# Source order for all engines and row pairs (gate, gate, value, value) from batch 2 on, in a fused attention, GLU and soft mixture-of-experts kernel

## The chip, the cores and the metric

The kernel runs on one core of a Trainium2 chip. The metric is the device time of one execution in microseconds (us). One execution was taken with the hardware profiler; all trace rows in this document are from that execution.

## What is computed

The reference has three parts, one behind the other. `B, H, S, Ns, D = 8, 8, 512, 32, 64`, all float32.

```python
# 1: cross reads between tokens x (B,H,S,D) and states (B,H,Ns,D)
a     = softmax(x @ state.T / sqrt(D), over states);  xread = a @ state
a2    = softmax(state @ x.T / sqrt(D), over tokens);  sread = a2 @ x
x     = concat([xread, sread], rows) as (4352 tokens, 512)
# 2: gated linear unit behind an RMS norm, d_ff = 1536
xn    = x / rms(x) * rms_g
h     = silu(xn @ w_gate) * (xn @ w_val);             x = h @ w_out
# 3: soft mixture of experts, 8 experts with 4 slots each
logits   = x @ phi
d        = softmax(logits, over tokens);  slot_in = d.T @ x
slot_out = relu(slot_in @ w1[e]) @ w2[e]   per expert
out      = softmax(logits, over slots) @ slot_out
```

## The kernel before

**Tiles and stages.** The 512 tokens of one batch element ("batch" below, 0 to 7) make one group `g` of four row tiles of 128. The kernel never forms `xread`: since `xread @ w = a @ (state @ w)`, it first multiplies the 32 states by a 512-column block of the gate or value weights (the state product, `sw`, line 531; its result is the tile `wp`, in a high and a low part), and then multiplies the attention weights `A` with it (`main_mm`, line 557). d_ff is cut into three blocks `c` of 512 columns. So a batch has 12 units `(g, c, t)`. A unit has a gate row and a value row of six matmuls each. ScalarE turns the gate row into `sg` (SiLU, `main_silu`, line 572), VectorE makes `h = value * rinv * sg` (`main_h`, line 577).

Stage 0 holds units of batches 0 and 1 and most of the weight preparation, stage 1 the rest of batch 1, stages 2 to 7 one batch each. Then come six halves for the 256 rows of `sread` (`w_split` at line 784 cuts weights for them into two parts on ScalarE and VectorE), the experts and the output. From stage 8 on the expert weights are streamed in.

**Small work between main rows.** In stages 2 to 7 the main rows stand in blocks of 24 matmuls (two units), and behind each block stands a burst of small work, written out by hand in `steady(g)`, bursts 0 to 5. It holds:

- `turn(c, t)` = `h_T` (line 586): four 128x128 transposes of `h` on TensorE into a `misc` bank, then a copy to `hT` on ScalarE, or on VectorE when the third argument is true. `lg_mm` (line 598) multiplies four turned tiles with `w_out @ phi` for the logits;
- `post1`, `post2`, `post_exp`, `post3`, `slot_h` (lines 622 to 705): the running softmax over tokens of the batch before. `post_exp` makes `E`, `post3` transposes `E` and `L`, `slot_h` adds to `acc`; `sacc` is the running sum (line 664). `c_exp`, `c_norm` (lines 707, 712) do the softmax over slots;
- `sw(g, c, gv)` for the blocks of columns that come next. Its two PSUM banks are emptied by a cast on ScalarE (line 545) and a subtraction on VectorE (line 546) each;
- the attention of the next batch `nb` and the one after it `nn`: `att_a3` (scores `sT`), `att_a4` (transposed scores `a`, maxima `rm`, `cm`, `ncm`), `att_exp`, `att_norm`, `att_b1` to `att_b4`, `att_z`, `att_gram`, `att_q`, `att_v`, `att_ss`, `rinv_from` (lines 225 to 526). `att_q`, `att_v`, `att_ss` and `rinv` give the RMS factor from the Gram matrix of the states;
- one piece of weight conversion (`wload`, `wconv`, lines 161 and 195): two ScalarE passes, three VectorE operations and one GpSimd addition per half, and a store.

Work for the other engines alone is put on units by `at(u, slot, f)`: slot 1 of unit `u` is run between its gate and value row, slot 2 behind its value row.

**Buffers.** PSUM has three banks `mm` for main rows, four banks `misc` for all small work and one bank `lg`. SBUF tiles of 8 KB a partition come from one pool `k8` with 19 buffers; attention tiles from `k4` with 5.

**What sets the order.** The framework takes instructions per engine from a heap by priority, so an engine's order can differ from the source. In stages 2 to 7 the order of TensorE alone is given by the source:

```python
pe_order.enter_context(tc.manual_schedule(engines={mybir.EngineType.PE}))
```

On the other engines only instructions marked with `tc.keep_in_program_order` keep their place (some ScalarE exponentials, `att_z`, `att_g`). All VectorE work and nearly all of ScalarE's, GpSimd's and the DMA queue's (SyncE) is placed by the heap. SyncE issues every load and store of these stages in one queue.

Of the kernel before, what the change touches and what calls it, by code (L numbers as in the profile page):

```python
# [20 lines left out]
def kernel(  # L21
# [87 lines left out]

    def transpose(o, i):  # L110
        nc.tensor.transpose(o, i, ident)  # L111
# [64 lines left out]
    def wconv_begin():  # L176
# [12 lines left out]
        if pinned:  # L189
            tc.keep_in_program_order(ins)  # L190
        ins = nc.scalar.activation(out=rnd, in_=lo.bitcast(U32), func=AF.Copy, scale=2.0 ** -29)  # L191
        if pinned:
            tc.keep_in_program_order(ins)
        begun.append((gv, c, j, d2, dst, hi, rnd))

    def wconv(n):
        for _ in range(n):
            if not begun:
                wconv_begin()
            gv, c, j, d2, dst, hi, rnd = begun.pop(0)  # L200
            a = dst.bitcast(I32)
            hs = [slice(0, 512), slice(512, 1024)]
            for h in hs:
                nc.vector.tensor_scalar(  # L204
                    out=dst[:, h], in0=dst[:, h], scalar1=EXP_LO, scalar2=EXP_HI,
                    op0=ALU.max, op1=ALU.min,
                )
                nc.vector.tensor_scalar(  # L208
                    out=a[:, h], in0=a[:, h], scalar1=3, scalar2=0x3FFFFFF8,
                    op0=ALU.logical_shift_left, op1=ALU.bitwise_and,  # L210
                )
                nc.vector.scalar_tensor_tensor(  # L212
                    out=a[:, h], in0=hi[:, h], scalar=-0x40000000, in1=a[:, h],
                    op0=ALU.bitwise_and, op1=ALU.bitwise_or,
                )
                nc.gpsimd.tensor_tensor(  # L216
                    out=a[:, h], in0=a[:, h], in1=rnd[:, h], op=ALU.add
                )
            if gv == 2:
                WOT[c, j] = d2  # L220
            if gv == 3:
                r0 = c * 512 + 2 * j * P
                nc.sync.dma_start(
                    out=w_out32[r0 : r0 + 2 * P, :].rearrange("(k p) d -> p k d", p=P), in_=d2
                )

    def att_g(b):
# [7 lines left out]
        if b > 0:  # L237
            tc.keep_in_program_order(ins)
# [26 lines left out]
    def att_a4(b):  # L265
        sT = T[b, "sT"]
        if b > 0:
# [11 lines left out]
            if b > 3:  # L279
                cm = T[b, "cm"]  # L280
                nc.vector.reduce_max(cm, sT, axis=AX.X)
                nc.vector.tensor_scalar(
                    out=T[b, "ncm"], in0=cm, scalar1=-scale, scalar2=None, op0=ALU.mult
# [333 lines left out]
    Q = {}  # L617
# [881 lines left out]
```

## Time and profile before

| | us |
|---|---|
| median of 3 runs | 665.63 |
| lowest and highest | 663.20, 666.14 |
| the profiled execution | 666.31 |
| its span, first to last instruction | 664.5 |
| TensorE busy | 615.8 (93%) |
| VectorE, ScalarE, GpSimd busy | 438.9 (66%), 346.5 (52%), 157.3 (24%) |
| mean granted TensorE clock | 0.961 |

The span is one execution on the chip; the profiled time has 1.8 us around it. Busy time of TensorE (PE) is a modelled number: matmuls overlap, so the distance from the start of one group of matmuls to the start of the next tells more than its busy share. The page's line of the granted clock shows full speed in nearly all slices between the start and the end of the kernel.

### The profile page before, as it was taken

Reading aid. Unit: us, or ns where it says so; the run is one execution under the profiler, and the core shown is the slowest. Engines: PE = TensorE matmul, PEld = TensorE weight load, DVE = VectorE, ACT = ScalarE, POOL = GpSimd, SP = SyncE. Lnnn points to the kernel's source line nnn. Section 1 sums busy time; section 2 is a strip of 40 time slices with the busy share of each in tenths; the row PEclk is TensorE's granted clock in tenths of the full one; section 3 lists DMA queues with packets and bytes.
Section 4 is the critical chain, followed back from the end, with each engine's and each line's share of the span. In section 5 each row is a group of like instructions: output and inputs, shape, how many; then the busy total and the mean of one; then the engine's idle time right before and its main releaser. Section 6 shows DMA issues by size and latency. Waiting matters only on the chain.

```text
span 664.5 us, 11190 instructions
## 1 busy us (share of the span) xinstructions
PE 615.8 (93%) x4432; PEld 387.5 (58%) x4432; DVE 438.9 (66%) x876; ACT 346.5 (52%) x552; POOL 157.3 (24%) x178
## 2 busy tenths in 40 slices
PE   6787989899998999999999999999999999999990
PEld 4435655356565566566656666666666777653350
DVE  6969899676578676856867685786765365252160
ACT  5457784475268447544844763484346476311170
POOL 2635464442031411401141041113000000003420
PEclk9588998899999999999999999999999999999996
DMA  9950064231020410041040104300270327999857
GB/s 354 417 206 1 1 241 190 77 127 51 18 62 35 163 33 33 1 163 64 1 154 14 60 1 159 128 1 34 92 288 3 126 86 269 312 337 396 311 205 332
DMA packets 32715, 92.14 MB, mean 139 GB/s; under 512 B 1816, under 2 KB 3224, under 8 KB 29848
## 3 DMA queue, kind: packets, MB, share of 16 engines
q1 hardware_dynamic: 32376, 91.36, 37.3%
q8 instruction: 35, 0.57, 0.3%
q14 instruction: 16, 0.13, 0.1%
q10 hardware_dynamic: 288, 0.07, 0.0%
HBM read 79.37 MB, written 12.06 MB: 138 GB/s over the span
## 4 chain that ended last, share of the span: by engine, by line
PE 75%; DVE 15%; ACT 5%; issue 2%; DMA 1%; POOL 0%; DVEq 0%; ACTq 0%
PE mm L85 43%; PE misc L85 18%; PE misc L111 9%; PE lg L85 3%; DVE w L204 2%; PE so L85 2%; DVE wp L546 2%; DVE w L212 2%; DVE h L582 1%; DVE w L208 1%; DVE wo L204 1%; DVE wo L212 1%; DMA raw_t<-in_w_gate_dram 1%; ACT hT L593 1%; ACT wp L545 1%
## 5 line engine op out<-in xcount | busy, mean ns | idle before, releaser
L85 PE MATMUL mm<-wp,A 128*128 128x512 f32 x1152 | 285.8, 400 | 2.9 <-DVE h L582 2.2
L85 PEld LDWEIGHTS mm<-wp,A 128*128 128x128 f32 x1152 | 213.3, 190 | 73.8 <-issue 23.8
L582 DVE SCALAR_TENSOR_TENSOR h<-mm,rinv,sg 128x512 f32<-128x512 f32 x102 | 76.0, 747 | 88.2 <-PE mm L85 82.0
L574 ACT ACTIVATE sg<-mm,rinv 128x512 f32<-128x512 f32 x102 | 70.7, 693 | 103.3 <-PE mm L85 88.9
L545 ACT CAST wp<-misc 128x512 fp32r<-128x512 f32 x96 | 51.5, 591 | 68.1 <-PE misc L85 68.1
L546 DVE TENSOR_TENSOR wp<-misc,wp 128x512 fp32r<-128x512 f32 x96 | 62.6, 684 | 23.2 <-ACT wp L545 22.8
L85 PE MATMUL misc<-w,stTg 64*32 64x512 f32 x768 | 67.7, 637 | 7.9 <-POOL w L216 5.1
L111 PEld LDWEIGHTS misc<-ident,h 128*128 128x128 f32 x408 | 44.9, 140 | 37.4 <-DVE h L582 13.9
L593 ACT COPY hT<-misc 128x512 f32<-128x512 f32 x81 | 45.3, 592 | 38.1 <-PE misc L111 32.4
L111 PE MATMUL misc<-ident,h 128*128 128x128 f32 x408 | 58.3, 279 | 5.8 <-DVE wp L546 5.1
L216 POOL TENSOR_TENSOR w<-w,raw 128x512 int32<-128x512 int32 x20 | 28.3, 1428 | 29.6 <-issue 7.3
L519 POOL TENSOR_TENSOR rinv<-ri,rs_magic 128x4 int32<-128x4 int32 (+1 forms) x9 | 1.8, 197 | 131.4 <-DVE ri L515 131.4
L85 PE MATMUL mm<-wh,xsg 128*128 128x512 f32 x96 | 31.8, 400 | 0.0
L216 POOL TENSOR_TENSOR wo<-wo,raw 128x512 int32<-128x512 int32 x18 | 24.7, 1384 | 22.6 <-DVE wo L212 7.0
L85 PEld LDWEIGHTS misc<-w,stTg 64*32 64x32 f32 x768 | 11.0, 107 | 31.4 <-issue 10.9
L476 POOL TENSOR_TENSOR A<-aT,A 128x1024 fp32r<-128x1024 f32 x7 | 16.9, 2408 | 47.5 <-ACT A L475 47.5
L85 PE MATMUL lg<-hT,wphi 128*32 128x512 f32 (+1 forms) x216 | 27.5, 579 | 0.0
L85 PE MATMUL misc<-h,ET 128*32 128x512 f32 x204 | 26.4, 596 | 0.0
L1245 POOL MEMSET sinE<- 128x512 f32 x2 | 1.0, 524 | 105.7 <-PE mm L85 95.6
L574 ACT ACT_TABLE_LOAD x18 | 23.1, 1283 | 0.8 <-PE mm L85 0.5
L191 ACT ACTIVATE raw<-raw 128x1024 int32<-128x1024 uint32 x19 | 21.9, 1155 | 0.0
L85 PEld LDWEIGHTS mm<-wh,xsg 128*128 128x128 f32 x96 | 17.9, 188 | 6.6 <-issue 3.1
(223 smaller groups left out, 852.6 us busy)
## 6 DMA issues: line engine op xcount, KB each, us to landing
ew<-in_w_dram SPq DMA_DIRECT2D x27, 1024.0 KB, 7.7
xT<-in_x_t_dram SPq DMA_DIRECT2D x8, 1024.0 KB, 7.4
xn<-in_x_n_dram SPq DMA_DIRECT2D x8, 1024.0 KB, 6.0
raw<-in_w_val_dram SPq DMA_DIRECT2D x6, 1024.0 KB, 15.8
raw<-in_w_out_dram SPq DMA_DIRECT2D x6, 1024.0 KB, 5.3
out_dram<-ob SPq DMA_DIRECT2D x6, 1024.0 KB, 10.7
ew_w<-in_w_dram SPq DMA_DIRECT2D x5, 1024.0 KB, 10.5
raw<-in_w_gate_dram SPq DMA_DIRECT2D x4, 1024.0 KB, 13.7
```

What stands on the lines that cost most here:

```text
L85: nc.tensor.matmul(out=o, lhsT=lhsT, rhs=rhs, start=start, stop=stop)
L111: nc.tensor.transpose(o, i, ident)
L191: ins = nc.scalar.activation(out=rnd, in_=lo.bitcast(U32), func=AF.Copy, scale=2.0 ** -29)
L204: nc.vector.tensor_scalar(out=dst[:, h], in0=dst[:, h], scalar1=EXP_LO, scalar2=EXP_HI, op0=ALU.max, op1=ALU.min,)
L212: nc.vector.scalar_tensor_tensor(out=a[:, h], in0=hi[:, h], scalar=-0x40000000, in1=a[:, h], op0=ALU.bitwise_and, op1=ALU.bitwise_or,)
L216: nc.gpsimd.tensor_tensor(out=a[:, h], in0=a[:, h], in1=rnd[:, h], op=ALU.add)
L476: nc.gpsimd.tensor_tensor(out=A[:, :, 1, :], in0=aT, in1=A[:, :, 0, :].bitcast(F32), op=ALU.subtract)
L545: nc.scalar.copy(t[:, r, 0, :], ps)
L546: nc.vector.tensor_tensor(out=t[:, r, 1, :], in0=ps, in1=t[:, r, 0, :].bitcast(F32), op=ALU.subtract)
L574: nc.scalar.activation(out=sg, in_=ps, func=AF.Silu, scale=RINV[g][:, t : t + 1])
L582: nc.vector.scalar_tensor_tensor(out=HH[g, c][:, t, :], in0=ps, scalar=RINV[g][:, t : t + 1], in1=sg, op0=ALU.mult, op1=ALU.mult,)
L593: (nc.vector.tensor_copy if on_dve else nc.scalar.copy)(HT[g, c][:, :, t * P : (t + 1) * P], ps.rearrange("p (q n) -> p q n", q=4))
```

## The change

From stage 2 to the end of stage 7, `manual_schedule()` without an engine list gives the order of every engine by the source; the single marks (`keep`) are off there. The two units of a block run gate, gate, value, value in place of gate, value, gate, value; slot 1 of the first unit now stands behind both gate rows and slot 1 of the second between the two value rows. In the bursts every `sw` moves to the end of its burst, each `turn` is paired, and `att_gram` goes from burst 0 to burst 1. `post_exp` and `c_exp` leave burst 0 for slot 1 of unit 2; `att_exp` goes from unit 1 to unit 0; `load_xt` from unit 8 to unit 5; `att_v` from burst 4 to unit 8; `att_z` and `att_a4` to unit 10; `c_norm` from unit 2 to unit 6; the weight conversion is cut in two halves, in burst 2 and at unit 6. Four functions are cut off others so that they can stand elsewhere: `att_cm`, `att_rs`, `post_sum`, `sread_split`; `sread_prep2` moves from the end of stage 6 to burst 0 of stage 7. No operation is added or removed.

The diff, cut to its core (the bodies of `wconv_half`, `att_cm`, `att_rs`, `post_sum` and `sread_split` are lines of the functions before):

```diff
+    by_hand = []
+    def keep(ins):
+        if not by_hand:
+            tc.keep_in_program_order(ins)
...
+    def wconv_half(i):
...
+    def att_cm(b):
+        cm = T[b, "cm"]
+        nc.vector.reduce_max(cm, T[b, "sT"], axis=AX.X)
+        nc.vector.tensor_scalar(
+            out=T[b, "ncm"], in0=cm, scalar1=-scale, scalar2=None, op0=ALU.mult
+        )
...
-            tc.keep_in_program_order(ins)
+            keep(ins)
+        if not by_hand:
+            att_rs(b)
...
         b = bursts[0]
         if g > 2:
             b += [(lg_mm, g - 1, 2, 3), (post1, g - 1)]
-        b += [turn(0, 0, True), (sw, g, 1, 0), (post2, g - 1)]
-        if not last:
-            b += [(att_gram, nb)]
-        b += [(post_exp, g - 1), (c_exp, g - 2, True)]
+        b += [turn(0, 0, True), turn(0, 1, True), (post2, g - 1), (sw, g, 1, 0)]
+        if last:
+            b += [(sread_prep2,)]
         b = bursts[1]
         if 2 < g < B - 1:
             b += [(att_b2, g)]
-        b += [(sw, g, 1, 1), turn(0, 1, True), (post3, g - 1), turn(0, 2)]
+        if not last:
+            b += [(att_gram, nb)]
+        b += [turn(0, 2, True), (post3, g - 1)]
         if not last:
             b += [(att_b1, nb)]
+        b += [turn(0, 3), (post_sum, g - 1), (sw, g, 1, 1)]
         b = bursts[2]
-        b += [turn(0, 3), turn(1, 0)] + [(slot_h, g - 1, i) for i in range(NC)]
+        b += [(slot_h, g - 1, i) for i in range(NC)]
+        if not last:
+            b += [(lg_mm, g, 0, 3)]
+        if g == B - 2:
+            b += [(att_b2, nb)]
         if 2 < g < B - 1:
             b += [(att_b3, g)]
-        if g == B - 2:
-            b += [(att_b2, nb)]
-        b += [(lg_mm, g, 0, 3), (sw, g, 2, 0)]
+        b += [turn(1, 0), turn(1, 1)]
+        if not last:
+            b += [(wconv_half, 0)]
+        b += [(sw, g, 2, 0)]
         b = bursts[3]
-        b += [(sw, g, 2, 1)]
         if not last:
             b += [(att_q, nb, 0), (att_q, nb, 1)]
-        b += [turn(1, 1), turn(1, 2)]
+        else:
+            b += [(lg_mm, g, 0, 3)]
+        b += [turn(1, 2), turn(1, 3)]
         if g == B - 2:
             b += [(att_b3, nb)]
+        b += [(sw, g, 2, 1)]
         b = bursts[4]
         if nn < B:
             b += [(att_a3, nn)]
-        b += [turn(1, 3)]
-        if not last:
-            b += [(att_v, nb), (att_ss, nb), (rinv, nb), (sw, nb, 0, 0)]
-        else:
-            b += [turn(2, 0)]
+        if last:
+            b += [(lg_mm, g, 1, 3)]
         if g == B - 2:
             b += [(sread_sum,)]
+        b += [turn(2, 0, True), turn(2, 1)]
+        if not last:
+            b += [(att_ss, nb), (rinv, nb)]
+        if not last:
+            b += [(sw, nb, 0, 0)]
         b = bursts[5]
         if not last:
-            b += [(sw, nb, 0, 1), turn(2, 0), (lg_mm, g, 1, 3), turn(2, 1), turn(2, 2), turn(2, 3, True)]
-            if g == B - 2:
-                b += [(sread_prep2,)]
+            b += [(lg_mm, g, 1, 3), turn(2, 2), turn(2, 3, True)]
+            if nn < B and nn > 3:
+                b += [(att_cm, nn)]
+            b += [(sw, nb, 0, 1)]
             ended.add(g)
         else:
-            b += [turn(2, 1), (lg_mm, g, 1, 3), turn(2, 2)]
+            b += [turn(2, 2)]
...
-        at(2, 1, c_norm, g - 2)
+        at(6, 1, c_norm, g - 2)
         if not last:
+            at(0, 1, att_exp, nb)
+            at(0, 1, wload, 1)
+            at(2, 1, att_rs, nb)
+            at(2, 1, att_norm, nb)
+        at(2, 1, post_exp, g - 1)
+        at(2, 1, c_exp, g - 2)
+        if not last:
+            at(4, 1, att_b4, nb)
+            at(4, 1, wconv_begin)
+            at(6, 1, wconv_half, 1)
+            at(6, 1, att_g, nb)
             at(1 if g == B - 2 else 7, 1, load_xn, nb)
-            at(1, 1, att_exp, nb, True)
-            at(2, 1, att_norm, nb)
-            at(4, 1, att_b4, nb)
-            at(6, 1, att_g, nb)
-            at(1, 1, wload, 1)
-            at(4, 1, wconv, 1)
+            at(8, 1, att_v, nb)
         if nn < B:
-            at(8, 1, load_xt, nn)
-            at(9, 1, att_z, nn)
-            at(11, 1, att_a4, nn)
+            at(5, 2, load_xt, nn)
+            at(10, 1, att_a4, nn)
+            at(10, 1, att_z, nn)
...
+            at(6, 1, sread_split)
             at(11, 1, w_split, 0, 0)
...
-                pe_order.enter_context(tc.manual_schedule(engines={mybir.EngineType.PE}))
+                by_hand.append(pe_order.enter_context(tc.manual_schedule()))
+                by_hand.append(1)
...
             if s > 1:
                 if u % 2:
-                    for f, *a in bursts[u // 2]:
+                    continue
+                pair = units[u : u + 2]
+                sgs = []
+                for k, (_, c, t) in enumerate(pair):
+                    ps = main_mm(g, c, t, 0)
+                    sgs.append(main_silu(g, c, t, ps))
...
+                for k, (_, c, t) in enumerate(pair):
+                    for f, a in plan.pop((base + u + k, 1), []):
                         f(*a)
+                    psv = main_mm(g, c, t, 1)
+                    main_h(g, c, t, psv, sgs[k])
...
+                    for f, a in plan.pop((base + u + k, 2), []):
+                        f(*a)
+                for f, *a in bursts[u // 2]:
+                    f(*a)
...
         if s == B - 1:
             pe_order.close()
+            by_hand.clear()
```

## Rows read from the trace of the kernel before

**Rows 1.** Stretches: start:end, length, busy PE, PEld, DVE, ACT, POOL, clock, DMA share, GB/s.
```profile
186.70:249.40 62.70, 60.53 (x433) 38.07 (x425) 48.95 (x98) 35.17 (x56) 16.52 (x14) 1.00 0.24 79
308.20:367.00 58.80, 58.11 (x461) 37.92 (x457) 42.07 (x84) 32.44 (x53) 11.87 (x11) 1.00 0.19 65
425.80:483.80 58.00, 57.23 (x510) 38.24 (x502) 40.38 (x84) 30.58 (x49) 8.80 (x8) 1.00 0.21 75
483.80:538.40 54.60, 54.00 (x353) 37.27 (x346) 29.18 (x65) 29.82 (x50) 0.20 (x1) 1.00 0.30 112
...
593.00:629.00 36.00, 35.48 (x316) 13.69 (x309) 7.96 (x32) 3.31 (x6) 11.71 (x35) 1.00 0.99 376
```

**Rows 2.** Timeline of TensorE in batch 4: start us, length us, line, tiles, count, [idle before].
```profile
327.00 0.27 PE L677 MATMUL misc<-ident,E 128*128 128x128 f32 x1
327.11 0.27 PE L678 MATMUL misc<-ident,L 128*128 128x128 f32 x1
327.99 0.66 PE L111 MATMUL misc<-ident,h 128*128 128x128 f32 x4 [0.60 <-DVE wp L546]
328.58 1.40 PE L111 MATMUL misc<-ident,sT 128*128 128x128 f32 x8
329.73 5.71 PE L85 MATMUL mm<-wp,A 128*128 128x512 f32 x24
335.28 1.03 PE L111 MATMUL misc<-ident,h 128*128 128x128 f32 x8
336.24 2.78 PE L85 MATMUL misc<-h,ET 128*32 128x512 f32 x24
...
340.21 1.09 PE L85 MATMUL misc<-w,stTg 64*32 64x512 f32 x16
341.23 5.74 PE L85 MATMUL mm<-wp,A 128*128 128x512 f32 x24
346.90 1.09 PE L85 MATMUL misc<-w,stTg 64*32 64x512 f32 x16
...
357.93 1.46 PE L85 MATMUL misc<-w,stTg 64*32 64x512 f32 x16
359.32 5.73 PE L85 MATMUL mm<-wp,A 128*128 128x512 f32 x24
```

**Rows 3.** The same view in batch 2.
```profile
200.91 5.98 PE L85 MATMUL mm<-wp,A 128*128 128x512 f32 x24
206.82 1.09 PE L85 MATMUL misc<-w,stTg 64*32 64x512 f32 x16
...
208.44 0.27 PE L678 MATMUL misc<-ident,L 128*128 128x128 f32 x1
210.80 0.65 PE L111 MATMUL misc<-ident,h 128*128 128x128 f32 x4 [2.08 <-DVE wp L546]
```

**Rows 4.** Waits of TensorE from 186.7 to 538 us: us in total, times, longest.
```profile
PE misc L111 <- DVE wp L546: 5.1, 6, 2.1
```

**Rows 5.** Timeline of ScalarE and VectorE behind the state product of 340.21.
```profile
341.34 1.08 ACT L545 CAST wp<-misc 128x512 fp32r<-128x512 f32 x2 [4.35 <-PE misc L85]
...
341.96 1.29 DVE L546 TENSOR_TENSOR wp<-misc,wp 128x512 fp32r<-128x512 f32 x2 [1.12 <-ACT wp L545]
```

**Rows 6.** Timeline of GpSimd and VectorE: a VectorE operation that overlaps one of GpSimd's.
```profile
323.42 1.92 POOL L337 TENSOR_TENSOR a<-a,asum 128x1024 f32<-128x1024 f32 x1
...
323.88 1.47 DVE L664 SCALAR_TENSOR_TENSOR sacc<-sacc,al,es 128x1 f32<-128x1 f32 x1 [0.24 <-ACT al L663]
```

**Rows 7.** Groups by line over the whole span: count, busy us, mean ns, idle before.
```profile
L270 DVE STREAM_TRANSPOSE a<-sT 128x1024 f32<-128x1024 f32 x7 | 8.7, 1240 | 0.6 <-ACT sT L258 0.6
L281 DVE TENSOR_REDUCE cm<-sT 128x2 f32<-128x1024 f32 x4 | 4.8, 1209 | 0.0
L310 ACT ACTIVATE sT<-sT,ncm 128x512 f32<-128x512 f32 x16 | 11.4, 714 | 1.5 <-DVE ra L522 1.4
L574 ACT ACT_TABLE_LOAD x18 | 23.1, 1283 | 0.8 <-PE mm L85 0.5
```

More of the change, by code (lines that the diff above doesn't have):

```diff
@@ L199, in wconv @@
                 wconv_begin()
[L200 to L225, printed above, removed]
+            for i in range(2):
+                wconv_half(i)
     def att_g(b):
@@ L663, in post_exp @@
             nc.scalar.activation(out=al[:np_], in_=dm[:np_], func=AF.Exp)
-            nc.vector.scalar_tensor_tensor(
-                out=sacc[:np_], in0=sacc[:np_], scalar=al[:np_], in1=es[:np_],
-                op0=ALU.mult, op1=ALU.add,
-            )
-            Q[g, "al"] = al
+            Q[g, "al"], Q[g, "es"] = al, es
+            if not by_hand:
+                post_sum(g)
         else:
@@ L671, in post_exp, with post_sum @@
         Q[g, "E"] = E
+    def post_sum(g):
+        np_ = gsize(g) * 32
+        nc.vector.scalar_tensor_tensor(
+            out=sacc[:np_], in0=sacc[:np_], scalar=Q[g, "al"][:np_], in1=Q[g, "es"][:np_],
+            op0=ALU.mult, op1=ALU.add,
+        )
     def post3(g):
@@ L710, in c_exp @@
         if pin:
[L711 removed]
+            keep(ins)
     def c_norm(g):
@@ new lines @@
+                for f, *a in bursts[u // 2]:
+                    f(*a)
+                pend = [units[-1]] if g == B - 1 and u == 10 else []
+                ps = None
+            else:
+                ps = main_mm(g, c, t, 0)
+            now = next_turned() if s < 2 else []
+            if s < 2:
+                sg = main_silu(g, c, t, ps)
+                for it in now:
+                    h_T(*it, on_dve=(s > 0 and u in (1, 2)))
+                run(1)
+                psv = main_mm(g, c, t, 1)
+                main_h(g, c, t, psv, sg)
+                for it in now:
+                    lg_mm(*it)
+                if ends(now):
+                    pg = now[-1][0]
+                    at(u, 2, post1, pg)
+                    if s < 2 and u + 1 < len(units):
+                        at(u + 1, 1, post2, pg)
+                        at(u + 1, 1, post_exp, pg)
+                        at(u + 2, 2, post3, pg)
+                        for i in range(NC):
+                            at(u + 4, 1, slot_h, pg, i)
+                run(2)
+                pend = pend[len(now) :] + [(g, c, t)]
@@ L1129 @@
+            if g == B - 2 and u == len(units) - 2:
                 att_ctx.__exit__(None, None, None)
```

81 lines of the change are left out of this document (44 added, 37 removed).

## The prediction

> **What bounds the kernel now.** I read the stretches by batch first: in batch 4 TensorE is busy 58.11 of 58.80 us, in batches 2, 6 and 7 60.53 of 62.70, 57.23 of 58.00 and 54.00 of 54.60, always at clock 1.00, while VectorE has 42.07 and ScalarE 32.44 us of work [rows 1]. So in stages 2 to 7 (186.7 to 538.4 us) the time is TensorE's own program, and batches 3, 4 and 5 are alike. Nothing can be won there but the places where TensorE stands still or does a group slower than it does the same group elsewhere. These are read from the second view, TensorE's timeline, by the distance from one group's start to the next.
>
> In batch 4 [rows 2] there are three.
> (a) The transpose at L678 starts at 327.11 and the next group at 327.99, 0.88 us; the equal transpose before it (L677) took 0.11. Loss 0.77. The releaser is VectorE's subtraction of `wp`: `sw(g, 1, 1)` stands at the head of burst 1, its two `misc` banks are emptied late, and the third tile behind it finds all four banks taken. That wait stands in each of the six batches [rows 4].
> (b) The eight transposes of `sT` take 1.15 us (328.58 to 329.73); the eight at 335.28 take 0.96. Loss 0.19, the tail of the same jam.
> (c) The state product at 357.93 takes 1.39, the one at 340.21 takes 1.02. Loss 0.37: again a bank.
> Sum 1.33 of 58.8. In batch 2 (a) is 210.80 - 208.44 - 0.11 = 2.25, and one block of main rows takes 5.91 in place of 5.67 [rows 2, 3].
>
> **The change part by part.**
> *Sums of instructions.* Nothing is added: each batch keeps its 461 matmuls, so TensorE's work changes only by neighbours. A lone `turn` takes 0.59 (327.99 to 328.58), two in a row 0.96, 0.48 each [rows 2]. Of twelve turns some four that stand alone get a neighbour: -0.4. Blocks behind a state product take 5.67 (341.23 to 346.90), the one behind transposes 5.55 (329.73 to 335.28) [rows 2]; in the new order nearly all stand behind a product: +0.1 in batches 2 to 6, +0.3 in batch 7, where three blocks stood behind transposes. Net -0.3, in batch 7 about 0.
>
> *`sw` to the end of the burst.* Its banks are then emptied beside a main block of 5.67 us, where TensorE takes no `misc` bank. That removes the cause of (a), (b) and (c). What is late next is the product itself. Behind the product of 340.21 the ScalarE cast starts 1.13 us after its start, the first subtraction after 1.75, and the second ends after 3.04 (341.96 + 1.29) [rows 2, 5]. A value row that stands next but two gate rows starts 1.02 + 5.67/2 = 3.86 after the product's start. Margin 0.8. With the old order (gate, value) it would be 1.02 + 1.42 = 2.44, too early; the new order of rows pays for the new place, so I cost the two together. Three bursts a batch (1, 3, 5) end with a value product that is needed at once.
>
> *The queues at these three places.* VectorE now runs in source order, so what stands ahead of the subtractions counts. Burst 1: three full-width operations (`h` and two copies) taken at 0.7 like a subtraction, five small ones at up to 0.4 and `sacc` at up to 1.47 [rows 5, 6] make 5.6 us at most, likely 4.6; the first subtraction can't start before 3.3 us of other TensorE work + 1.75 = 5.0 us after the block. Late by 0.6 at most, within the margin. Burst 3: `h` and three operations of `att_q`, four times 0.7, 2.8 us, against 2.5 + 1.75 = 4.2. Burst 5 is the tightest: behind burst 4's product VectorE has `rinv` (estimated at 2.4 us: eleven small operations at 0.2 and a trip to GpSimd), two subtractions (1.3), `att_a4` (1.24 for a transpose like L270's, and a maximum of about 1.2 like L281's), two `h`, a copy and `att_cm` (1.21) [rows 7]. Laid out from the end of the block before, VectorE is free at 13.05 us, the cast allows 12.7, so the second subtraction ends at 14.3 and the value row wants it at 14.8. It fits by about 0.5 us. I cost all three at nothing; the cover is two gate rows, 2.84 us.
>
> *ScalarE.* `att_exp` and then `post_exp` with `c_exp` stand behind both gate rows of units 0 and 2. Each cluster costs a table load there and one back, 1.28 us each [rows 7], four a batch as before. The longer cluster has two passes of 0.71 and one of twice the size [rows 7]: 1.28 + 4 x 0.71 = 4.1 us at most; it ends about 7.6 us into the batch; the next cast wants ScalarE at about 9. `E` is ready some 2 us before `post3`, where batch 2 lacked it. Cost nothing.
>
> *GpSimd and VectorE.* What the rows show: `sacc` takes 1.47 us for one element a partition, and ends with GpSimd's pass over `a` (323.42 + 1.92 = 325.34) [rows 6]. In the new order `sacc` (`post_sum`) stands some 2 us behind that pass. I count no gain, since VectorE isn't the bound. The Trainium skill, "SBUF — State Buffer", section "Who interferes with whom", says why such an operation stands still: VectorE and GpSimd share one pair of ports, and who starts first holds it for its whole instruction. The row agrees; a sum by that rule differs only where GpSimd comes to stand ahead of VectorE at one of the three places, which is the first rival.
>
> *DMA queue.* SyncE's order is now the source's too: `wload`, `xT` and `stT`, the store of the converted weights, `xn`. `xT` goes ahead of the store and needs a `k8` buffer three units earlier; counted through a batch, at most 18 of 19 are held. Each load has over 10 us until it is needed. Cost nothing; if a buffer were short, the loads behind would be late by up to a block, 5.7 us, once a batch, still covered by those 10 us.
>
> *Buffers of burst 1.* It takes eight `misc` banks in about 4.3 us, with four banks. Each must be emptied within some 2 us; a copy is about 0.7. Bound from below 0; from above one copy in each burst, 0.7 x 6 = 4.2 us a batch. By the order of readers the bank wanted is free 0.1 to 0.8 us ahead each time, so I take 0.2 a batch.
>
> *Sum.* Batch 2: 2.25 + 0.19 + 0.37 + 0.24 + 0.3 = 3.35. Batches 3 to 5: 3 x (1.33 + 0.3) = 4.9. Batch 6 has (a) and (b) but (c) not: 0.96 + 0.3 = 1.25; batch 7 (a) alone: 0.75. Together 10.25; less 6 x 0.2 = 1.2 for new bank waits: 9.0. Behind 538 us the stages keep their code. The weights stream there at DMA share 0.99 from 593 to 629 [rows 1], but each load starts when a buffer is given free by TensorE's work, so the stretch moves as a whole. The profiled execution took 666.3 us, 0.7 above the median of 665.63: 657.3 for such a one, and 656.6 for the median.
>
> **The rivals.**
> *1. VectorE late at the three places, slower.* In strict source order one held-up operation ahead of the subtractions delays the value row. The price: 6 batches x 3 places less the two that batch 7 lacks, 16, each at (lateness - 0.8). The gain is gone at 9.0/16 + 0.8 = 1.4 us; a GpSimd pass that holds VectorE up for its whole 1.92 us [rows 6] at each place gives 16 x 1.1 - 9.0 = +8.9, so 674.5. For it: such holds are in the trace, and burst 5 has 0.5 us to spare. Against it: by the order laid out, GpSimd's long passes fall in the main blocks. 0.1.
> *2. The wait only moves.* Pairs of turns and products at the ends could jam the four banks in most bursts by 0.25 us: 6 x 6 x 0.25 = 9.0, so 665.6, no change. For it: eight tiles through four banks in burst 1; against it: VectorE's copies are no later than before. 0.13.
> *3. The last stages give part of it back.* If the weight stream (share 0.99) didn't start earlier, PE would wait for it; half the gain would go, 661. For it the 0.99; against it that each load waits for a buffer, not for the clock. 0.1, still faster.
> *4. The change doesn't do what it says:* the heap's order was nearly the source's, and only the bursts move. Then TensorE's order, which the source gave before, still brings the gain; I fold this into the forecast, with no chance of its own.
>
> **How the numbers follow.** Forecast, 656.6, 0.67; rivals 1, 2 and 3 have 0.1, 0.13 and 0.1. A measurement of this kernel can tell about 0.5%, 3.3 us, from no change: faster means below 662.3. Forecast less 0.02 and rival 3 lie there: 0.75; same is rival 2 and that 0.02, 0.15; slower is rival 1, 0.10. The range goes from 653, all 10.25 and a little for a calmer VectorE, to 665, which takes in rival 3 and half of rival 2; outside are rival 1 and the rest of 2.
>
> **What would show it.** Right: no wait of TensorE at L678, batches 3 to 5 near 57.2 us each, batch 2 near 59.5, every state product 1.02 long, all at clock 1.00, and the stretch from the end of stage 7 to the end as long as before (126 us). Wrong: TensorE waiting for `wp` (VectorE L546) ahead of value rows (rival 1); idle time ahead of transposes or products released by ScalarE or VectorE copies (rival 2); waits of matmuls for weight loads behind 580 us (rival 3).

## The result and the profile after

| | before | after |
|---|---|---|
| median of 4 runs, us | 665.50 | 657.67 |
| lowest and highest | 663.20, 666.14 | 655.60, 660.28 |
| ratio, 95% interval | | 0.9893 [0.9869, 0.9917] |
| profiled execution, its span | 666.31, 664.5 | 655.60, 653.8 |
| TensorE busy | 615.8 (93%) | 613.1 (94%) |
| VectorE, ScalarE, GpSimd busy | 438.9, 346.5, 157.3 | 436.9, 338.5, 157.8 |

Two later sets of six runs of the changed kernel gave 0.9898 [0.9876, 0.9920] and 0.9884 [0.9857, 0.9912]. The forecast was 656.6 with a range of 653 to 665: the time and the sign were right. The way to it was right in part only, as the stages show. One thing is to be added to "The change": the third argument of `turn` becomes true for two turns a batch, so 33 of the 102 copies to `hT` run on VectorE now, where 21 did before. A stage is measured here from the first main matmul of one batch to the first of the next (the last one to the first matmul of the `sread` halves). First the kernel before, by these borders: start:end, length, busy PE, PEld, DVE, ACT, POOL, granted clock, DMA share, GB/s.

```profile
0.00:191.14 191.14, 166.38 (x1128) 100.08 (x1128) 148.96 (x282) 111.27 (x164) 77.22 (x66) 0.89 0.38 146
191.14:251.28 60.14, 57.97 (x403) 37.67 (x402) 45.72 (x86) 33.71 (x56) 16.52 (x14) 1.00 0.26 89
...
310.09:368.88 58.79, 58.10 (x461) 37.93 (x459) 42.07 (x82) 32.43 (x53) 11.87 (x11) 1.00 0.19 65
...
487.20:536.88 49.68, 49.08 (x313) 33.69 (x312) 25.70 (x60) 25.09 (x42) 0.20 (x1) 1.00 0.26 96
536.88:664.46 127.58, 109.33 (x709) 63.01 (x706) 51.17 (x122) 46.58 (x86) 18.97 (x56) 0.96 0.80 293
```

The same view of the changed kernel; these lines answer to [rows 1].

```profile
0.00:186.38 186.38, 165.32 (x1128) 98.89 (x1128) 147.53 (x282) 111.15 (x164) 78.66 (x66) 0.91 0.41 155
186.38:244.52 58.14, 57.49 (x404) 37.89 (x402) 43.84 (x86) 32.27 (x52) 16.23 (x14) 1.00 0.22 75
...
302.07:359.59 57.52, 57.39 (x466) 38.33 (x458) 41.52 (x85) 31.52 (x50) 11.71 (x11) 1.00 0.19 66
...
475.49:526.18 50.69, 50.42 (x323) 34.12 (x315) 27.32 (x62) 23.64 (x41) 0.20 (x1) 1.00 0.28 107
526.18:653.80 127.62, 109.38 (x709) 63.01 (x706) 51.86 (x123) 46.33 (x85) 18.98 (x56) 0.95 0.80 293
```

Read the two side by side:

- **Ahead of batch 2** the two programs issue the same instructions in the same order on TensorE, VectorE, ScalarE and GpSimd (the counts in the two first lines agree); only the last two loads of the DMA queue differ. And yet this stretch is 4.76 us shorter in the second profile, and 4.74 of that is there before those loads: `xn` is loaded at 137.92 us in the first and at 133.18 in the second. So 4.76 of the 10.7 us between the two profiled spans is not the change's.
- **Batches 2 to 7**, at clock 1.00 in both, take 345.74 us before and 339.78 after: 5.96 us less. Batch by batch, from 2 to 7: -2.00, -1.26, -1.27, -1.26, -1.16 and +1.01. This is what the change does, and it was forecast at 9.0. (The prediction's signs "batch 2 near 59.5" and "126 us" go by the borders of [rows 1]. By the borders used here its sum gives 57.0 for batch 2 and 57.4 for batches 3 to 5; the 57.2 given there leaves the 0.2 for bank waits out.)
- **The end**, from the `sread` halves on, is 127.58 and 127.62 us, equal.

TensorE's timeline of batch 4 answers to [rows 2]: start, length, engine, line, tiles, count. L677 and L678 of before are L696 and L697 here, L111 is L117.

```profile
307.73 1.06 PE L85 MATMUL lg<-hT,wphi 128*32 128x512 f32 x8
308.72 1.09 PE L117 MATMUL misc<-ident,h 128*128 128x128 f32 x8
309.75 0.43 PE L85 MATMUL misc<-lgs,r 128*32 128x128 f32 x8
310.10 1.16 PE L85 MATMUL misc<-w,stTg 64*32 64x512 f32 x16
311.20 5.74 PE L85 MATMUL mm<-wp,A 128*128 128x512 f32 x24
...
318.00 0.66 PE L117 MATMUL misc<-ident,h 128*128 128x128 f32 x4
318.50 0.27 PE L696 MATMUL misc<-ident,E 128*128 128x128 f32 x1
318.61 0.27 PE L697 MATMUL misc<-ident,L 128*128 128x128 f32 x1
318.71 1.04 PE L117 MATMUL misc<-ident,sT 128*128 128x128 f32 x8
319.59 0.60 PE L117 MATMUL misc<-ident,h 128*128 128x128 f32 x4
320.26 1.23 PE L85 MATMUL misc<-w,stTg 64*32 64x512 f32 x16
321.42 5.74 PE L85 MATMUL mm<-wp,A 128*128 128x512 f32 x24
...
349.75 1.18 PE L85 MATMUL misc<-w,stTg 64*32 64x512 f32 x16
350.85 5.76 PE L85 MATMUL mm<-wp,A 128*128 128x512 f32 x24
```

L696 and L697 now follow each other at 0.11 and 0.10 us: the 0.77 is gone. The eight `sT` transposes take 0.88 from start to start (1.15 before). The products take 1.10, 1.16 and 1.10 at these three places, where a free one takes 1.02: the second half of each starts only when a copy out of a bank has ended (for the first, VectorE's copy to `hT` at 310.16; for the second, ScalarE's to `e2T` at 320.38). Over batches 2 to 7 the waits of TensorE that the view lists are one line, in place of the 5.1 us of [rows 4]:

```profile
PE misc L117 <- DVE h L596: 0.8, 2, 0.5
```

Last, VectorE at the place that the prediction called the tightest, the end of burst 5:

```profile
359.27 1.21 DVE L310 TENSOR_REDUCE cm<-sT 128x2 f32<-128x1024 f32 x1
...
360.59 1.28 DVE L560 TENSOR_TENSOR wp<-misc,wp 128x512 fp32r<-128x512 f32 x2
```

The second subtraction ends at 361.87. The block starts at 359.59, so its value rows begin half a block, 2.83 us, later, at 362.42. Margin 0.55; the prediction had laid out 0.5.

### The profile page after: what moved, and what is told of

Same layout as the page of the kernel before. It is cut to its first block, busy times and chain, and to the rows that moved or that the text cites. A ratio compares the mean times of both kernels' runs of the same rounds, so it can differ in the third digit from the quotient of the medians.

```text
span 653.8 us, 11181 instructions
## 1 busy us (share of the span) xinstructions
PE 613.1 (94%) x4432; PEld 388.5 (59%) x4432; DVE 436.9 (67%) x888; ACT 338.5 (52%) x538; POOL 157.8 (24%) x178
## 4 chain that ended last, share of the span: by engine, by line
PE 77%; DVE 8%; ACT 1%; issue 1%; POOL 0%; DVEq 0%; ACTq 0%
PE mm L85 45%; PE misc L85 17%; PE misc L117 10%; PE lg L85 4%; PE so L85 2%; DVE w L206 1%; DVE h L596 1%; DVE wo L214 1%; DVE w L214 1%; DVE wp L560 1%; DVE w L210 0%; DVE wo L206 0%; DVE wo L210 0%; DVE rinv L539 0%; ACT sg L588 0%
## 5 line engine op out<-in xcount | busy, mean ns | idle before, releaser
L607 ACT COPY hT<-misc 128x512 f32<-128x512 f32 x69 | 38.2, 588 | 90.7 <-PE misc L117 84.9
L85 PE MATMUL misc<-w,stTg 64*32 64x512 f32 x768 | 68.4, 627 | 9.3 <-POOL w L218 6.2
L117 PEld LDWEIGHTS misc<-ident,h 128*128 128x128 f32 x408 | 45.3, 140 | 23.0 <-DVE h L596 16.8
L117 PE MATMUL misc<-ident,h 128*128 128x128 f32 x408 | 56.6, 277 | 1.4 <-DVE h L596 1.4
L351 POOL TENSOR_TENSOR a<-a,asum 128x1024 f32<-128x1024 f32 x7 | 13.4, 1916 | 68.4 <-DVE asum L350 64.0
L607 DVE COPY hT<-misc 128x512 f32<-128x512 f32 x33 | 22.1, 683 | 10.2 <-PE misc L117 10.0
```

Source lines behind the costliest of these rows:

```text
L85: nc.tensor.matmul(out=o, lhsT=lhsT, rhs=rhs, start=start, stop=stop)
L351: (eng or nc.gpsimd).tensor_tensor(out=a3, in0=a3, in1=asum.unsqueeze(2).to_broadcast([P, 32, 32]), op=ALU.mult)
L607: (nc.vector.tensor_copy if on_dve else nc.scalar.copy)(HT[g, c][:, :, t * P : (t + 1) * P], ps.rearrange("p (q n) -> p q n", q=4))
```

## The experiments

The stages of all profiles, in us, measured as above. "Ahead" is the stretch to the first main matmul of batch 2.

| kernel | ahead | 2 | 3 | 4 | 5 | 6 | 7 | 2 to 7 | end |
|---|---|---|---|---|---|---|---|---|---|
| before | 191.14 | 60.14 | 58.81 | 58.79 | 58.81 | 59.51 | 49.68 | 345.74 | 127.58 |
| the change | 186.38 | 58.14 | 57.55 | 57.52 | 57.55 | 58.35 | 50.69 | 339.78 | 127.62 |
| e0_change_again | 186.06 | 58.15 | 57.54 | 57.52 | 57.52 | 58.35 | 50.67 | 339.75 | 127.63 |
| e12_change_timed_beside | 190.41 | 58.15 | 57.50 | 57.50 | 57.50 | 58.31 | 50.66 | 339.62 | 127.61 |
| e1_tensor_order_only | 186.30 | 61.96 | 61.53 | 61.50 | 61.52 | 60.96 | 50.30 | 357.77 | 128.14 |
| e5_old_bursts_all_order | 189.21 | 70.06 | 68.88 | 68.45 | 68.37 | 69.95 | 51.16 | 396.88 | 127.52 |
| e3_products_first | 189.28 | 58.89 | 58.86 | 58.81 | 58.83 | 59.56 | 50.98 | 345.92 | 127.62 |
| e2_old_row_order | 186.93 | 59.09 | 58.12 | 58.13 | 58.13 | 61.83 | 52.07 | 347.38 | 127.86 |
| e6_cm_twice | 190.47 | 58.12 | 57.70 | 57.73 | 57.71 | 58.51 | 50.66 | 340.42 | 127.64 |
| e7_cm_three_times | 191.32 | 58.15 | 58.98 | 58.95 | 58.98 | 59.81 | 50.66 | 345.54 | 127.61 |
| e9_split_pair | 191.68 | 58.22 | 57.57 | 57.56 | 57.57 | 58.37 | 51.57 | 340.86 | 127.62 |
| e8_two_bursts | 189.48 | 57.55 | 57.53 | 57.51 | 57.55 | 58.31 | 50.14 | 338.58 | 127.62 |
| e10_four_bursts | 190.52 | 57.50 | 57.39 | 57.39 | 57.39 | 57.97 | 50.06 | 337.69 | 127.62 |
| e11_four_bursts_timed | 186.39 | 57.47 | 57.38 | 57.38 | 57.38 | 57.97 | 50.08 | 337.66 | 127.56 |

**The change again.** No edit, for e0 and for e12.

> The change once more, timed. Theory: the first 186 to 191 us (up to the first main row of batch 2) are the same instructions in the same order as before, and the 4.8 us that this stretch differed by between the two profiles is the clock's, not the change's; so the stretch comes out anywhere from 184 to 192 us again, while batch 2 takes 58.1, batches 3 to 5 57.5 each, batch 6 58.3, batch 7 50.7 and the rest 127.6 us to 0.1 us each. Ratio to the kernel before near 1 - 6.0/665 = 0.991. Rival: the change made the first stretch faster too; then it is near 186.4 again and the ratio near 0.984.

> The change itself, in the same five rounds on the same chip. Its stages 2 to 7 should be 339.7 to 339.8 us again, and its ratio to the kernel before near 0.989.

Medians 657.99 and 656.15 of six runs each, beside 665.79 and 664.37 of the kernel before. Every stage from batch 2 on came again within 0.05 us, but the stretch ahead is 186.38, 186.06 and 190.41 in three profiles of one kernel. The 186.06 of e0 alone would have fitted the rival too; the 190.41 of e12 rules it out.

So a total carries some 5 us that no edit made, and an edit of batches 2 to 7 is read from their own lengths.

**The order of TensorE alone.** The new bursts and rows stay; the other engines go back to the heap, without the single marks that the kernel before has.

```diff
-                by_hand.append(pe_order.enter_context(tc.manual_schedule()))
+                by_hand.append(pe_order.enter_context(tc.manual_schedule(engines={mybir.EngineType.PE})))
```

> The changed bursts and rows, but only TensorE in source order; VectorE, ScalarE, GpSimd and the DMA queue are placed by the heap, without single marks. Theory (the place of the state products and the row order free the misc banks, the order of the other engines only has to be no worse): batches 3 to 5 within 0.4 of 57.5 us, the wait behind the transposes of E and L gone. Rival (the source order of the other engines is what removes the waits): batches 3 to 5 at 58.5 us or more, with waits of TensorE for VectorE or ScalarE.

673.99 us, batches 3 to 5 at 61.5: slower than before by 2.7 a batch. TensorE's waits over batches 2 to 7 have a line that neither kernel has:

```profile
PE mm L85 <- DVE wp L560: 6.7, 4, 1.7
```

VectorE in batch 4, where TensorE's value row stood from 333.50 until 335.17 for it:

```profile
330.97 0.68 DVE L560 TENSOR_TENSOR wp<-misc,wp 128x512 fp32r<-128x512 f32 x1
331.57 2.94 DVE L210 TENSOR_SCALAR wo<-wo 128x512 int32<-128x512 int32 x2
334.44 0.68 DVE L560 TENSOR_TENSOR wp<-misc,wp 128x512 fp32r<-128x512 f32 x1
```

Two passes of weight conversion, 2.94 us, stand between the two subtractions that the value row wants. The heap puts them there; the source's order doesn't. This is the first rival's wait, made by the heap instead of by the source order. It is half of the 13.4 us for which TensorE stands in batches 2 to 7; the rest are shorter waits for `h` (3.7), `sg` (1.7), `e2T` (1.0) and `E` (0.3).

**The order of all engines, with the old bursts.** The kernel before, with its bursts and rows, and the source's order on every engine.

```diff
-                pe_order.enter_context(tc.manual_schedule(engines={mybir.EngineType.PE}))
+                by_hand.append(1)
+                pe_order.enter_context(tc.manual_schedule())
```

(and the helper `keep`, so that the single marks are off, as in the change)

> The kernel before with nothing changed but the order: from batch 2 on all engines in source order, with the old bursts and the old rows. Theory (source order of the other engines and the new bursts with products at their ends only pay together; the heap loses 4 us a batch with the new bursts): the old source stands each exponential and the running sum right behind the small work that feeds it, so VectorE and ScalarE stand in front of work that is ready; batches 3 to 5 at 59 to 62 us, no better than 58.8. Rival (the source order of the other engines alone removes the wait behind E and L): batches 3 to 5 at 57.4 to 58.2 us.

715.4 us, ten a batch over the kernel before in batches 2 to 6, and so further off than the theory had it. Not all of it is waiting: TensorE stands for 42.3 us, and in batches 2 to 6 the granted clock is at half for 10.2, 6.8, 3.4, 3.4 and 3.4 us, where the other kernels of the table have full clock in batches 2 to 7 (but for e2's batch 6). The largest wait is TensorE's for `h`: 21.7 us in five, up to 4.4. VectorE ahead of one of them, in batch 4 (TensorE stood 4.32 us until 360.78):

```profile
354.65 1.71 DVE L210 TENSOR_SCALAR wo<-wo 128x512 f32<-128x512 f32 x1 [2.50 <-ACT wo L194]
...
359.37 0.69 DVE L218 SCALAR_TENSOR_TENSOR wo<-raw,wo 128x512 int32<-128x512 int32 x1
359.98 1.40 DVE L588 SCALAR_TENSOR_TENSOR h<-mm,rinv,sg 128x512 f32<-128x512 f32 x2
```

VectorE first waits 2.50 us for ScalarE's part of the weight conversion, then does its six operations, and two `h` stand behind them in the source's order. In burst 0 of that batch it stands 4.11 us before the sums `rs` of the exponentials. The change cuts the conversion in two halves and puts those sums a unit later (`att_rs`): that these cuts are what makes the source's order bearable is read off the waits and wasn't tried by itself. With e1 this makes a table of four, us per batch 3 to 5: old bursts and heap 58.8, old bursts and source order 68.4 to 68.9, new bursts and heap 61.5, both new 57.5. Neither half of the change helps alone, as far as tried: the new bursts under a heap with the single marks were not run.

**Products back at the head.** All else of the change stays.

```diff
-        b += [turn(0, 0, True), turn(0, 1, True), (post2, g - 1), (sw, g, 1, 0)]
+        b += [(sw, g, 1, 0), turn(0, 0, True), turn(0, 1, True), (post2, g - 1)]
...
+        b += [(sw, g, 1, 1)]
         if not last:
             b += [(att_gram, nb)]
```

(and the same for the products of bursts 2 to 5)

> As the change, with all six state products of a batch moved back to the head of their bursts (behind att_b2 in burst 1). Theory: the banks jam again in burst 1 as before the change, 0.5 to 1.0 us behind the transposes of E and L or of sT, and a little in bursts 0, 4 and 5: batches 3 to 5 at 58.2 to 59.0 us. Rival (the place of the products does nothing, the order of the other engines does all): batches 3 to 5 within 0.2 of 57.5 us.

664.61 us; batches 3 to 5 at 58.81 to 58.86, to 0.05 us those of before. The bank waits are back, at other groups:

```profile
PE misc L85 <- DVE wp L560: 4.8, 12, 0.5
PE misc L696 <- DVE wp L560: 2.8, 5, 0.6
PE misc L117 <- DVE wp L560: 1.4, 6, 0.6
```

Their sum over batches 2 to 7 is 9.0 us, more than the 5.1 of the kernel before, so it is not just the old loss come back, though the lengths agree. With everything else new, the place of the product is what the gain hangs on, and the cause is the emptying of its banks, as predicted.

**Rows gate, value, gate, value again.**

```diff
-                for k, (_, c, t) in enumerate(pair):
-                    for f, a in plan.pop((base + u + k, 1), []):
-                        f(*a)
+                    if k == 1:
+                        for kk in range(2):
+                            for f, a in plan.pop((base + u + kk, 1), []):
+                                f(*a)
                     psv = main_mm(g, c, t, 1)
```

> All engines in source order and the new bursts, but the rows of a pair run gate, value, gate, value again; the work of slot 1 of both units stands between the second gate and the second value row. Theory as in the prediction (the row order pays for the place of the products): the value row behind bursts 1, 3 and 5 stands 2.4 us behind the start of its product, the last subtraction ends after 3.0; up to 0.6 us of waiting three times a batch, so batches 3 to 5 at 58.5 to 59.3 us. Rival: each part of the product is ready just before the matmul that reads it (the low part of the second half is read 0.7 us into the row), so no wait at bursts 1 and 3: batches 3 to 5 at 57.4 to 57.9 us.

664.15 us, batches 3 to 5 at 58.13: 0.6 more than the change, between what the two theories gave. (By "seam" is meant here the place where a value row reads the product that the burst ahead of it has just made: bursts 1, 3 and 5.) In batch 4 the value rows don't wait at three seams. The first block and the product of burst 3 are long, both by the distance to the next line:

```profile
304.15 6.04 PE L85 MATMUL mm<-wp,A 128*128 128x512 f32 x24
310.12 1.07 PE L85 MATMUL lg<-hT,wphi 128*32 128x512 f32 x8
...
343.12 1.37 PE L85 MATMUL misc<-w,stTg 64*32 64x512 f32 x16
344.42 5.75 PE L85 MATMUL mm<-wp,A 128*128 128x512 f32 x24
```

5.97 in place of 5.67 behind burst 5's product, and a product of 1.30 in place of 1.02: 0.58, nearly the whole difference. The first is in the first value row of the block, so the row order pays at one seam a batch, burst 5's, the one laid out as the tightest, and there 0.3. The second is no seam but a bank: the second half of burst 3's product starts at 343.43, when a copy to `hT` has ended (343.38). With the old rows 0.66 of the 1.27 that batch 4 gained would be left. Batches 2, 6 and 7 lose 0.95, 3.48 and 1.38 to the change; TensorE stands there for `sq` (1.9 us), `h` (1.2) and `E` (1.2), and 3.4 us of batch 6 from 470.6 on are at half clock. These weren't taken apart.

**VectorE made late.** The maximum `cm`, ahead of burst 5's subtractions, is repeated with the same outcome, twice in all in e6 and three times in e7.

```diff
-        nc.vector.reduce_max(cm, T[b, "sT"], axis=AX.X)
+        for _ in range(3):
+            nc.vector.reduce_max(cm, T[b, "sT"], axis=AX.X)
```

> The change with the column maximum in att_cm (1.21 us of VectorE, ahead of the subtractions of the last product of batches 2 to 5) done twice, with the same outcome. Theory (the value row has 0.55 us left when the second subtraction ends, and reads its result only 0.7 us into the row, 1.25 in all): no wait, batches 2 to 5 longer by 0 to 0.15 us. Rival (the 0.5 us that the prediction laid out is all there is): 0.6 to 0.8 us longer each.

> The same done three times: 2.42 us more of VectorE ahead of the last product. Theory: 2.42 - 1.25 = 1.2 us of waiting in the first value row of batches 3 to 6, each batch longer by 1.0 to 1.4. Rival of the prediction (VectorE late at such a place costs its lateness less 0.8): 1.6 us each. A third outcome, no wait, would mean that the value row isn't what the product is late for.

A repeat takes 1.24 us (3.72 for three). Batches 3 to 6 rise by 0.15 to 0.21 with one and by 1.43 to 1.46 with two. The waits of e7, TensorE's over batches 2 to 7:

```profile
PE mm L85 <- DVE wp L561: 4.1, 4, 1.0
```

Both lie a little over what the theory gave (0 to 0.15 and 1.0 to 1.4). The price is one for one beyond a margin: 1.24 - 0.17 and 2.48 - 1.44 give 1.07 and 1.04 us. It is larger than the 0.55 measured to the start of the value row, since that row's first matmul takes the cast part of `wp`, and the subtracted halves are wanted by its second and fourth (in e7 TensorE stands its 1.0 us ahead of the second). The first rival's mechanism is real, and its price was right but for the margin, 1.05 in place of 0.8. In the change VectorE just isn't late.

**A pair of turns split.** The two turns of burst 3 are taken apart, one ahead of `att_q` and one behind it.

```diff
         b = bursts[3]
+        b += [turn(1, 2)]
         if not last:
             b += [(att_q, nb, 0), (att_q, nb, 1)]
...
-        b += [turn(1, 2), turn(1, 3)]
+        b += [turn(1, 3)]
```

> The change with one pair of turns taken apart again: in burst 3 the first turn stands ahead of att_q and the second behind it. It measures the term of the prediction that a turn saves 0.1 us by standing beside another. By that term batches 3 to 5 take 57.54 + 0.1 = 57.64 us. Theory after the result (a group pays for the kind of matmul that stands ahead of it, so what counts is how often the kind changes, here once more): 0.1 to 0.3 us more, 57.64 to 57.84. Rival: no cost within 0.05 us.

Batches 3 to 5 at 57.57: 0.02 to 0.04 more than the change, where the prediction's credit was 0.1 for a turn that gets a neighbour. In batch 4 `att_q` and the two turns take 2.35 us together (343.81 to 346.16), 2.33 in the change (338.39 to 340.72): at this place there is no such credit.

Batch 7 rose by 0.9. There the turn at the head of burst 3 waits for its `h`:

```profile
515.88 0.66 PE L117 MATMUL misc<-ident,h 128*128 128x128 f32 x4 [0.92 <-DVE h L596]
```

In batches 3 to 5 the same turn stands straight behind the block that makes its `h` too, and doesn't wait. In batch 7 `h` itself is late: `sread_split` stands ahead of it in VectorE's order and waits for ScalarE first.

```profile
513.94 1.23 DVE L801 TENSOR_TENSOR xsg<-xg,xsg 128x1024 fp32r<-128x1024 f32 x1 [0.70 <-ACT xsg L800]
515.08 1.40 DVE L596 SCALAR_TENSOR_TENSOR h<-mm,rinv,sg 128x512 f32<-128x512 f32 x2
```

So a turn at the head of a burst has no cover when VectorE is late with its `h`.

**Two bursts repaired.** In batch 2's burst 0, `post2` goes ahead and the product between the two turns; in batch 7's burst 1 the last turn goes behind the product.

```diff
+        if g == 2:
+            b += [(post2, g - 1), turn(0, 0, True), (sw, g, 1, 0), turn(0, 1, True)]
...
+        if last:
+            b += [(post_sum, g - 1), (sw, g, 1, 1), turn(0, 3)]
```

> The change with two bursts rearranged: in batch 2, burst 0 begins with post2 and one turn, and the second turn goes behind the product (there the turn waited 0.5 us for its h, since no logit matmuls stand ahead of it); in batch 7, burst 1 has the product ahead of its second turn (there it waited 0.4 us for its h). Theory: batch 2 at 57.5 to 57.8 us in place of 58.15, batch 7 at 50.2 to 50.4 in place of 50.7, all else alike; the sum of batches 2 to 7 at 338.8 to 339.1 in place of 339.75. Rival: the wait moves to the next copy, no change.

Batch 2 fell by 0.60 to 57.55 and batch 7 by 0.54 to 50.14, and the other stages stayed; the sum, 338.58, is a little under what was expected. TensorE has no listed wait left. The two waits for `h` (0.49 and 0.27) and the neighbours changed with them were 0.60 of the 1.15 by which batch 2 fell short of the forecast and 0.54 of the 1.55 of batch 7. The ratio of six runs to the kernel before, 0.9904 [0.9881, 0.9927], can't be told from the change's 0.9898.

**Four bursts.** On top of e8: from batch 3 on the product of burst 0 ahead of `post2`, and up to batch 6 `att_ss` ahead of burst 4's turns.

```diff
-            b += [turn(0, 0, True), turn(0, 1, True), (post2, g - 1), (sw, g, 1, 0)]
+            b += [turn(0, 0, True), turn(0, 1, True), (sw, g, 1, 0), (post2, g - 1)]
...
+        if not last:
+            b += [(att_ss, nb)]
         b += [turn(2, 0, True), turn(2, 1)]
...
-            b += [(att_ss, nb), (rinv, nb)]
+            b += [(rinv, nb)]
```

> The version with the two rearranged bursts, and two more: from batch 3 on burst 0 has post2 behind the state product (128x32 tiles behind the product took 0.24 us before the change, 0.36 behind transposes now), and burst 4 has att_ss right behind att_a3, ahead of the turns (where it and the product behind it lost some 0.15 us). Theory: batches 3 to 5 at 57.2 to 57.4 us in place of 57.53, batch 6 at 58.1 to 58.2. Rival: the order of the kinds only moves the cost to the next group, or post2 late on VectorE makes E late: 57.5 us or more.

> The kernel of the four reordered bursts again, timed in five rounds beside the change and the kernel before. If what the stages show counts in the whole, its stages 2 to 7 are again 337.7 us in sum, 2.1 less than the change's 339.8, and its median lies 1 to 3 us below the change's of the same rounds, with the ratio to the kernel before near 0.986. If the first 190 us differ from run to run by more than that, the two medians lie within 1 us of each other in either direction, though the stages keep their 2.1.

Batches 3 to 5 fell to 57.39, batch 6 to 57.97, and batches 2 to 7 to 337.69 and 337.66 in two profiles: 2.1 below the change, 8.1 below the kernel before. Burst 0 in batch 4 of e10:

```profile
313.10 1.09 PE L85 MATMUL misc<-w,stTg 64*32 64x512 f32 x16
314.12 0.42 PE L85 MATMUL misc<-lgs,r 128*32 128x128 f32 x8
314.47 5.78 PE L85 MATMUL mm<-wp,A 128*128 128x512 f32 x24
```

The product is back at 1.02 from 1.10, but `post2` still takes 0.35, so its length isn't set by what stands ahead, as had been supposed. What stands behind it fits better: in the kernel before it takes 0.24 in batch 4, ahead of `att_gram`, but 0.36 in batch 7 (495.45 to 495.81), ahead of main rows as here. That wasn't tried by itself. The trace shows no listed wait of TensorE from batch 2 to 7 in e10. Timed, it has a median of 655.13 and a ratio of 0.9872 [0.9842, 0.9902]; the change beside it 656.15. It is the fastest of all: against the change beside it by 1.0 us in the medians, where the two intervals overlap, and by 2.0 in the stages, where batches 3 to 5 differ by 0.12 and repeat to 0.01 in its two profiles.

## Why the prediction was right, and where not

**The total.** The forecast gain was 9.0 us, the medians moved by 7.8, the stages by 5.96. The 3.0 us missing in the stages are 1.15 in batch 2, 0.5 in batches 3 to 5 together and 1.55 in batch 7 (batch 6 gave 0.1 more than forecast). So two thirds of the forecast gain were made. That the median came to within 1.1 us of the forecast is in part luck: some 1.9 us of the 7.8, by subtraction, are not from batches 2 to 7, the only ones that the change touches. The ratio that the stages alone would give, 0.991, lies inside the intervals of all three sets of runs. Only one profile of the kernel before is there, so whether its stretch ahead is longer on average, or the medians fell so, stays open.

**Batch 4, term by term**, by starts:

| term | forecast | measured |
|---|---|---|
| (a) wait at the second transpose of `post3` | -0.77 | -0.77 |
| (b) `sT` transposes | -0.19 | -0.27 |
| (c) products, and new bank waits | -0.37 + 0.2 | -0.07 |
| twelve turns and six blocks | -0.4 + 0.1 | +0.07 + 0.08 |
| other small groups | 0 | -0.31 |
| sum | -1.43 | -1.27 |

(a) and (b) hold, and e3 shows the cause. Of (c), the product of 1.39 became 1.10, but burst 0's and burst 1's went from 1.02 to 1.10 and 1.16; "every state product 1.02 long" was wrong, and what was put down as new bank waits is just this: 0.30 of the 0.37 did not come. (The 461 matmuls that the prediction gives each batch are those of batches like 4; batch 2 has 403 and batch 7 313, which no sum used.)

**The step that failed: "of twelve turns some four that stand alone get a neighbour: -0.4".** The turns got slower by 0.07. The sum counted what lone turns win and not what a row of three loses, and it counted one neighbour too many: before there were five lone turns, two pairs and a row of three, after it five pairs and, in burst 1, two that still stand alone ("each `turn` is paired" in "The change" is not right for these). At the prediction's own prices, 0.59 alone and 0.48 in a pair, with the 1.28 of the row of three, that makes 6.15 before and 5.98 after: -0.17 and not -0.4. That row, in the timeline of the kernel before:

```profile
366.59 1.07 PE L85 MATMUL lg<-hT,wphi 128*32 128x512 f32 x8
367.59 1.53 PE L111 MATMUL misc<-ident,h 128*128 128x128 f32 x12
368.87 0.48 PE L85 MATMUL mm<-wp,A 128*128 128x512 f32 x1
```

Three turns in 1.28, 0.43 each; the change breaks them up. The other 0.24 are the prices: its pairs behind `lg_mm` or `att_a3` take 1.02 (three of five), as 308.72 to 309.75 shows, and only behind other groups 0.97, and the lone turns take 0.49 and 0.67. The price of 0.96 for a pair was one row's, taken for all. What came in uncounted, -0.31, is in the main the other small groups (`slot_h`, `att_q`, `att_b2` and the transpose of `srd` shorter by 0.09 to 0.13 each, `post2` longer by 0.11); why these changed wasn't tried.

**Batch 2: the wait for `h` was not looked for.** The wait at L678 (2.24), `sT`, the products and the blocks fell as forecast (-3.0 in sum), but the turns rose by 0.92. In burst 0 there is no `lg_mm` ahead of the pair in batch 2, and the second turn comes before its `h`:

```profile
194.04 0.60 PE L117 MATMUL misc<-ident,h 128*128 128x128 f32 x4
195.12 0.66 PE L117 MATMUL misc<-ident,h 128*128 128x128 f32 x4 [0.49 <-DVE h L596]
195.71 0.43 PE L85 MATMUL misc<-lgs,r 128*32 128x128 f32 x8
```

With rows gate, gate, value, value both `h` of a block end at the block's end, so a turn at the head of a burst needs something ahead of it. I had looked at who waits for the product and not at who waits for the later `h`. e8 shows it: other neighbours, -0.60. The wait itself is 0.49 of the 0.92; the rest is in the lengths of the other turns.

**Batch 7** lost 1.01 where a gain of 0.55 was forecast: the wait at L678 fell by 0.33 only (0.27 of it came back as a wait for `h`), the turns rose by 0.47, and `sread_prep2`, moved there from batch 6, brought 0.47. That move I had not costed. Without it batch 6 gained about 0.8.

**The three seams.** Taken at nothing with a margin of 0.5 at the tightest; measured 0.55 to the row and 1.05 to the wait (e6, e7). Rival 1 (674.5) fell for that reason; that its time is near that of e1 (673.99), where the heap, not the source, made VectorE late, is chance. That "the new order of rows pays for the new place" was right at one of the three seams and for 0.3 us (e2).

**Rival 2** (the wait only moves) fell at its price of 1.5 us a batch: 0.8 us of listed waits in six batches, and in batch 4 the 0.30 of the longer products, which are waits for a bank. **Rival 3** (the end gives back) fell: 127.58 against 127.62 us, at DMA share 0.80 in both; the stretch moved as a whole. **Rival 4** was folded into the forecast with "TensorE's order, which the source gave before, still brings the gain". That was wrong: e1 has TensorE's new order alone, and it lost 12 us in batches 2 to 7. The heap's order is not nearly the source's, and the gain needs the order on the other engines; I had costed it at nothing instead of asking what the heap would do with the new bursts.

**`sacc`**, held in [rows 6] for 1.47 us beside a GpSimd pass, has none beside it after:

```profile
320.62 0.21 DVE L687 SCALAR_TENSOR_TENSOR sacc<-sacc,al,es 128x1 f32<-128x1 f32 x1
```

In the kernel before, the same operation takes 1.43 to 1.47 in batches 2 to 6, each time beside that pass, and 0.22 in batch 7 with none beside it. The Trainium skill, "SBUF — State Buffer", section "Who interferes with whom", says that the port pair shared by the two engines is an exclusive lock, and that a VectorE instruction with two inputs in SBUF contends with a GpSimd instruction that reads SBUF; these rows agree with it. One row of e1 doesn't: 0.21 us at 206.25, though a GpSimd operation is shown from 205.92 to 206.53 (its spans are rough). The end of the hold won no time, as forecast, since TensorE didn't wait for it.

## What to carry to other kernels

When groups of an engine's work are moved, find for each of them what waits for it and also the producer that it now stands too close to: here the products were freed and the first turns ran into `h`. An order of the work and the order of the engines that feed it are to be costed together; each half alone lost 2.7 or 10 us a batch (a part of the 10 at half clock) where both won 1.3. Compare stages, not totals, when the code ahead of the change is the same: these repeated to 0.05 us while the stretch ahead of them moved by 5.

## What the runs showed that was not expected

**The first 190 us.** With the same instructions in the same order on the four compute engines (but for e1, where some of the last ones differ) they took 186.06 to 191.68 us over the fourteen profiles. The granted clock in them falls to half (1.2 of 2.4 GHz) at different times. The kernel before:

```profile
0.00:15.00 15.00, 9.97 (x64) 7.05 (x64) 8.54 (x18) 8.34 (x12) 3.89 (x9) 1.00 0.89 344
15.00:38.90 23.90, 17.64 (x64) 8.96 (x65) 18.75 (x30) 10.32 (x17) 11.66 (x9) 0.50 1.03 419
```

The changed kernel:

```profile
0.00:15.50 15.50, 10.01 (x64) 7.31 (x64) 8.61 (x19) 8.46 (x13) 4.30 (x9) 1.00 0.89 345
15.50:32.60 17.10, 11.38 (x40) 6.69 (x41) 16.58 (x27) 8.24 (x12) 9.96 (x8) 0.50 1.02 418
```

The clock falls after 15 us in which TensorE was busy for ten, and the half-clock stretch lasts 23.9 us in one and 17.1 in the other. It isn't the length of all such stretches that decides: they add up to 34.1 us in the profile of 186.38 and to 27.3 in that of 190.41. Which of them falls where TensorE is the bound wasn't tried.
